# A fused retention and two-expert-layer kernel on one core: expert 0's raw-weight sums by ScalarE, PSUM and VectorE, x sums two a step, values asked for earlier, expert 3 staged by PSUM

## The chip, the cores and the metric

The kernel runs on one core of a Trainium2 chip. The metric is the device time in microseconds (us) of one execution. A core has five engines that each work through a queue of their own in order: TensorE (PE: matmuls, with its weight loads shown apart as PEld), VectorE (DVE), ScalarE (ACT), GpSimd (POOL) and SyncE (SP, which only issues transfers here). They share the on-chip buffer SBUF; matmuls write into PSUM.

## The reference, cut to what matters

Three layers follow on each other: causal retention, a dense layer of four experts, and a layer in which each token goes to the best of eight experts.

```python
def _attn_ref(q, k, v):                       # 4 x 8 heads x 576 x 64
    scores = scale * np.matmul(q, k.transpose(0, 1, 3, 2))
    Dmat = np.where(rel >= 0, gamma[:, None, None] ** rel[None, :, :], 0.0)
    return np.matmul(scores * Dmat[None, :, :, :], v)
def _moe_ref(x, domain_probs, w1, w2):        # x 2304 x 512, w1 4 x 512 x 1024
    p = domain_probs / (domain_probs.sum(-1, keepdims=True) + 1e-09)
    for e in range(E):
        out += p[:, e:e + 1] * (np.maximum(x @ w1[e], 0.0) @ w2[e])
def _moe2_ref(x, w_gate, w_output_gate, w1, w2):   # w1 8 x 512 x 1024
    logits = x @ w_gate; e_idx = np.argmax(logits, axis=1)
    gate_w = softmax(logits)[np.arange(N), e_idx]
    eom = 1.0 / (1.0 + np.exp(-(x @ w_output_gate)))
    for e in range(E):
        mask = e_idx == e
        out[mask] = gate_w[mask] * eom[mask, e] * (np.maximum(x[mask] @ w1[e], 0.0) @ w2[e])
```

## The kernel before, in words

**Numbers.** The expert layers multiply in f16. Each f32 value is split into a rounded f16 part `hi` and the f16 rest `lo = value - hi`, and a product takes three matmuls: hi x hi, hi x lo, lo x hi. The retention steps multiply in f32.

**Retention, 36 steps.** The sequence is cut into chunks of 64 tokens: 4 batches x 9 chunks are 36 steps. A step (`at_step`) multiplies the past state by the queries (L278), the next step's scores (L255, masked into `pf` by DVE, L260), `pf` by the values (L287), and makes the next state from `ks`, the keys weighted by POOL (`at_split`, L234), by the matmul L302. DVE adds the state up (`at_sum`, `sn`, L319) and scales the output into `xf` (L336); ACT writes its `hi` (L338), POOL its `lo` (L340; DVE, L342, for the first block). Queries, keys and values come by two transfers a step (`at_load`: `qkr`, `vkr`), four steps ahead in the opening, three later on.

**Blocks of x.** Four steps make a block of 256 tokens; there are nine. Each block also needs four differences of its quarters (`x_mix`, L348, POOL), which are split in their turn (`x_keep`: ACT L357, POOL L358, in two halves) and stored with the block (`x_store`, a POOL transfer, L361). A later part reads them back (`x_load`).

**The dense layer.** Expert 0 takes blocks 0 to 4 in the plain form (`l1_first`, L520, with `ht` by L506 on ACT and L507 on DVE; `l2`, L672, summing in PSUM tiles `po` of tag "o"). Everything later uses a seven-product form of the 2x2 block product: `l1_mixed` (L548) and `l2_mixed` (L633), whose seven products are added into `acc` by DVE (L641, weighted by `p_sb`), and whose left operands `op` get their `lo` from POOL (`whole`, L567). A block is up to 14 units of TensorE work. For the seven products the weights of an expert need sums and differences of their quarters: `mix`, L451, POOL, 16 per expert, made in place in the raw tile `wr`, between the splits `put` (`split_z`: ACT copies into a PSUM tile `pz`, L205, rounds it, L206, DVE subtracts, L207). Expert 0's sums are made while its own blocks 0 to 4 run.

**Hooks.** Between the units of expert 0 a hook runs one retention step (`at_hook`; steps 6 to 11 in block 0, eight each in blocks 1 to 3, four in block 4), `w_plan` runs one item of the list of weight sums and splits, and `s_plan` stages the second expert layer's weights: 128 pieces are read, split, and written back to DRAM as f16 pairs. For 46 of them `split_p` does it (L195, L196 on ACT, the difference L197 on POOL), for 82 `split_z`; expert 3's are by `split_p`. PSUM tiles `pz` are of tag "h" (shared with `ph`) or "o" (shared with `po`), two buffers each (`z_from`). From expert 3 on, the gating of the finished blocks runs too: `g1_rows` (L207 into `xr`), `g2` (L757), `g3a` (L767 to L774: maximum, key, one-hot), `g3b` (from L782; L808, L814), small DVE instructions of 128x16.

**Order.** A scheduler of the framework puts the instructions into each engine's queue; `pace` and `issue_after` hold the side work behind a given instruction of the main work. Within an engine the queue is strict.

```python
def split_p(raw, hi, lo, scale):
    act.activation(out=raw, in_=raw, func=ACTF.Copy, scale=scale)
    act.activation(out=hi, in_=raw, func=ACTF.Copy)
    pool.tensor_tensor(out=lo, in0=raw, in1=hi, op=ALU.subtract)
def split_z(raw, hi, lo, scale):
    z = z_at["bank"]().tile([128, 512], F32, tag=z_at["tag"], name="pz")
    act.activation(out=z, in_=raw, func=ACTF.Copy, scale=scale)
    act.activation(out=hi, in_=z, func=ACTF.Copy)
    dve.tensor_tensor(out=lo, in0=z, in1=hi, op=ALU.subtract)
```

Of the kernel before, what the change touches and what calls it, by code (L numbers as in the profile page):

```python
# [130 lines left out]
def kernel(  # L131
# [80 lines left out]
    at_ctx = ExitStack()  # L212
    at_raw = at_ctx.enter_context(tc.tile_pool(name="at_raw", bufs=4))
# [129 lines left out]

    def x_mix(b):

        m = xfs[b]
        for (ox, oy), x, y in (((0, 0), (1, 0), (0, 0)), ((1, 0), (1, 1), (1, 0)), ((1, 1), (1, 1), (0, 0)), ((0, 1), (0, 1), (1, 1))):
            pool.tensor_tensor(out=m[:, ox, oy], in0=m[:, x[0], x[1]], in1=m[:, y[0], y[1]], op=ALU.subtract)  # L348

    def x_keep(b):  # L350
        m = xfs.pop(b)
        if xos[b][1] is None:
            xos[b][1] = at_1.tile([128, 2, 4, 2, HB], F16, name="xm", bufs=1)
        with tc.issue_after(pace["act"].ins):
            for i in range(2):
                hi, lo = [xos[b][1][:, a, 2 * i:2 * i + 2] for a in range(2)]
                act.activation(out=hi, in_=m[:, i], func=ACTF.Copy)  # L357
                pool.tensor_tensor(out=lo, in0=m[:, i], in1=hi, op=ALU.subtract)  # L358

# [3 lines left out]
    def at_step(s):  # L363
# [10 lines left out]
        if s + 2 < NSTEP:
            at_split(s + 2)

    def at_done(s, f, *args):
        if s >= 0 and s % NS == NS - 1 and s < NSTEP:
            f(s // NS, *args)

# [772 lines left out]
    def at_hook():  # L1153
        s = nxt[0]
        if s >= NSTEP + 4:
            return
# [69 lines left out]
    def s_plan(e, b, u):  # L1226
        if e == 0 and b <= BM:
            if b == BM and u in (0, 2, 4, 6):
                s_hook()
        elif b >= 2:  # L1230
            if u in ((6, 13), (0, 3, 5, 7, 9), (0, 3, 5, 7, 9), (3, 5, 7, 9))[e] or u == 12 and (e == 3 and b < 5 or 0 < e < 3 and b >= 3):
                s_hook(split_z if 0 < e < 3 else split_p)
        elif b == 1 and u in (4, 6, 9):
            s_hook()

# [205 lines left out]
```

## Time and profile before

Three runs took 1009.95, 1010.9 and 1012.07 us, median 1010.9. The profiled execution took 1004.67 us; its span (first to last instruction of the trace) is 1002.9 us, its mean granted clock of TensorE 0.994.

| engine | busy us | share of the span | instructions |
|---|---|---|---|
| PE | 959.9 | 96% | 13507 |
| PEld | 825.7 | 82% | 13507 |
| DVE | 566.4 | 56% | 1251 |
| ACT | 525.6 | 52% | 1001 |
| POOL | 463.8 | 46% | 478 |

The page also cuts the span into 40 slices of 25.07 us, with each engine's busy share in tenths (9 is 90% or more). TensorE stands at 9 from the fourth slice on, until the last; in the first slices it is lower, and POOL is busiest there. Expert 0's plain blocks run in about the first 190 us, expert 3's blocks 3 to 7 begin at 633.27, 653.86, 674.46, 695.04 and 714.10 us, and the second expert layer ends the span. A releaser, named behind an arrow, is what ended the idle time in front of an instruction.

### The profile page before, as it was taken

The numbers are of one execution on the slowest core, as the hardware profiler recorded it, in microseconds if no ns is written. First come the engines' busy times: TensorE is split into PE (matmuls) and PEld (weight loads), VectorE is DVE, ScalarE is ACT, GpSimd is POOL, SyncE is SP. The second block draws the span as 40 slices with busy tenths as digits, with TensorE's granted clock in tenths as the row PEclk, the third lists the DMA queues.
The fourth block names the chain that finished last, engine by engine and source line by source line (L and its number), as shares of the span: only waits on it lengthen the run. The fifth ranks groups of instructions, "written<-read, shape, count | busy, mean of one in ns | idle before, by whom it ended". The sixth has DMA issues, their size and how long they took to land. (4 is left out here: it accounts for less than half of the span.)

```text
span 1002.9 us, 31867 instructions
## 1 busy us (share of the span) xinstructions
PE 959.9 (96%) x13507; PEld 825.7 (82%) x13507; DVE 566.4 (56%) x1251; ACT 525.6 (52%) x1001; POOL 463.8 (46%) x478
## 2 busy tenths in 40 slices
PE   5889999999999999999999999999999999999995
PEld 5566677899999999999999999888988677777773
DVE  5645461465677776766777774888798211211210
ACT  4235352677767777776787686576633122212221
POOL 3798973655555244454442554666543212112111
PEclk9999999999999999999999999999999999999998
DMA  9869884345457678476668636778945616554691
GB/s 343 291 221 324 269 269 156 108 119 185 164 187 219 224 260 275 122 212 215 207 195 318 226 96 164 207 214 235 222 143 202 232 44 220 203 227 143 255 397 44
DMA packets 95940, 209.49 MB, mean 209 GB/s; under 512 B 21486, under 2 KB 42222, under 8 KB 93488
## 3 DMA queue, kind: packets, MB, share of 16 engines
q1 hardware_dynamic: 82784, 159.20, 48.1%
q0 software_dynamic: 13008, 48.20, 15.0%
q8 instruction: 108, 1.77, 0.7%
q14 instruction: 40, 0.33, 0.1%
HBM read 197.88 MB, written 52.99 MB: 250 GB/s over the span
## 5 line engine op out<-in xcount | busy, mean ns | idle before, releaser
L633 PEld LDWEIGHTS <-op 128*128 128x128 f16 x2604 | 245.7, 98 | 30.3 <-issue 4.6
L567 POOL TENSOR_TENSOR op<-sm,op 128x512 f16<-128x512 f32 x124 | 142.2, 1157 | 180.2 <-ACT op L566 175.7
L548 PEld LDWEIGHTS <-wm_a 128*128 128x128 f16 x3264 | 192.8, 98 | 4.8 <-issue 1.0
L548 PE MATMUL ph<-xc,wm_a 128*128 128x128 f16 x2112 | 132.1, 219 | 0.0
L566 ACT ACTIVATE op<-sm 128x512 f16<-128x512 f32 x124 | 77.5, 633 | 83.6 <-DVE sm L571 83.6
L1055 DVE SCALAR_TENSOR_TENSOR h_s<-p_h,h_s 128x512 f16<-128x512 f32 x40 | 27.7, 692 | 158.4 <-ACT h_s L1054 151.2
L1062 PE MATMUL p_y<-wm_a,h_s 128*128 128x512 f16 x480 | 107.2, 379 | 0.5 <-DVE h_s L1055 0.5
L633 PE MATMUL pv<-wm_a,op 128*128 128x256 f16 x792 | 97.4, 273 | 0.0
L633 PE MATMUL px<-wm_a,op 128*128 128x256 f16 x744 | 91.5, 273 | 4.9 <-DVE acc L641 4.9
L451 POOL TENSOR_TENSOR wr<-wr 128x512 f32<-128x512 f32 x64 | 81.1, 1276 | 31.7 <-ACT pz L205 29.2
L1062 PEld LDWEIGHTS <-h_s 128*128 128x128 f16 x480 | 46.7, 98 | 52.4 <-DVE h_s L1055 0.7
L1065 POOL DMA_INDIRECT out_dram<-y_s,sidxm x17 | 17.2, 1014 | 146.4 <-ACT y_s L1064 137.8
L197 POOL TENSOR_TENSOR s<-sr,s 128x512 f16<-128x512 f32 x46 | 52.8, 1157 | 66.4 <-ACT s L196 62.2
L548 PEld LDWEIGHTS <-wm_b 128*128 128x128 f16 x1296 | 76.9, 98 | 1.4
L1054 ACT ACTIVATE h_s<-p_h 128x512 f16<-128x512 f32 x40 | 23.9, 597 | 78.5 <-PE p_h L1045 76.5
L641 DVE SCALAR_TENSOR_TENSOR acc<-px,p_sb,acc 128x256 f32<-128x256 f32 x124 | 59.2, 477 | 8.0 <-PE px L633 7.8
L1064 ACT ACTIVATE y_s<-p_y,x_g 128x512 f32<-128x512 f32 x20 | 13.7, 687 | 92.5 <-PE p_y L1062 74.3
L1045 PEld LDWEIGHTS <-wm_b 128*128 128x128 f16 x1056 | 59.9, 98 | 2.3
L1045 PE MATMUL p_h<-x_s,wm_b 128*128 128x128 f16 x1056 | 61.2, 219 | 0.0
L205 ACT ACTIVATE pz<-wr 128x512 f32<-128x512 f32 x100 | 59.4, 609 | 1.3 <-DVE wm_a L207 0.9
L207 DVE TENSOR_TENSOR s<-pz,s 128x512 f16<-128x512 f32 x82 | 54.7, 683 | 9.3 <-ACT s L206 9.3
L207 DVE TENSOR_TENSOR wm_a<-pz,wm_a 128x512 f16<-128x512 f32 x62 | 42.0, 689 | 28.8 <-ACT wm_a L206 27.9
(206 smaller groups left out, 1848.8 us busy)
## 6 DMA issues: line engine op xcount, KB each, us to landing
wm_a<-w2d SPq DMA_DIRECT2D x20, 2048.0 KB, 9.0
wr<-in_w_dram SPq DMA_DIRECT2D x40, 512.0 KB, 6.3
wm_b<-w1d SPq DMA_DIRECT2D x10, 2048.0 KB
wm_a<-w1d SPq DMA_DIRECT2D x10, 2048.0 KB
sr<-in_w1s_dram SPq DMA_DIRECT2D x64, 256.0 KB, 3.5
w1d<-s SPq DMA_DIRECT2D x64, 256.0 KB, 4.9
sr<-in_w2s_dram SPq DMA_DIRECT2D x64, 256.0 KB, 4.8
w2d<-s SPq DMA_DIRECT2D x64, 256.0 KB, 5.1
```

Source lines behind the costliest of these rows:

```text
L197: pool.tensor_tensor(out=lo, in0=raw, in1=hi, op=ALU.subtract)
L205: act.activation(out=z, in_=raw, func=ACTF.Copy, scale=scale)
L207: dve.tensor_tensor(out=lo, in0=z, in1=hi, op=ALU.subtract)
L451: pace["pool"] = pool.tensor_tensor(out=quarter(e, n, k, to), in0=quarter(e, n, k, x), in1=quarter(e, n, k, y), op=op)
L548: pe.matmul(bank[:, i], lhsT=w[:, k, u, 128 * i:128 * i + 128], rhs=x[:, v, d, k], start=(first and i == 0 and n == 0), stop=(n == 5), ski ...
L566: act.activation(out=hi, in_=s, func=ACTF.Copy)
L567: pool.tensor_tensor(out=lo, in0=s, in1=hi, op=ALU.subtract)
L633: pe.matmul(out, lhsT=o[a][:, v, k], rhs=w[c][:, k, u], start=(first and n == 0), stop=(n == 11), skip_group_check=True,)
L641: step = dve.scalar_tensor_tensor(out=a, in0=src, scalar=p_sb[:, b * TB + i, e:e + 1], in1=a, op0=ALU.mult, op1=ALU.add)
L1045: pe.matmul(ph[:, j], lhsT=w[k][:, x, f * 128:(f + 1) * 128], rhs=xs[:, y, k], start=(n == 0), stop=(n == 3 * KD - 1),)
L1055: dve.scalar_tensor_tensor(out=lo, in0=ph, scalar=0.0, in1=hi, op0=ALU.max, op1=ALU.subtract)
L1062: pe.matmul(po, lhsT=h[:, a, k], rhs=w[k][:, b], start=(n == 0), stop=(n == 3 * KF - 1))
```

## The change

1. `mix` for expert 0 no longer adds on POOL: ACT copies one quarter into a PSUM tile of the current tag, DVE adds or subtracts the other. Sixteen of the 64 sums.
2. `x_mix` makes two of its four differences a step, in the two steps behind the block's last; `x_keep` makes its two halves in the two steps after that, and the second store follows. `ago` counts the steps. The first block's, which stood at the end of the opening, come in the hooks of steps 6 to 10.
3. Values are asked for four steps ahead (`load_vk`, five buffers), queries and keys three (`load_qk`, four buffers); `at_split` stands ahead of `at_step` in the hook.
4. Expert 3's pieces of the staging (29) are split by `split_z`, and one of a block's hooks stands at unit 1 in place of 12. Expert 0's and those of block 1 of experts 1 to 3 stay with `split_p`.

```diff
+    def load_vk(s):
+        b, c = divmod(s, NC)
         t = at_raw.tile([128, 10, D], F32, name="vkr")
-        sp.dma_start(out=a[:, 0:10 if c else 8], in_=qk[b, c][:, 0:10 if c else 8])
...
-    def x_mix(b):
+    def x_mix(b, i):
...
+        for (ox, oy), x, y in steps[2 * i:2 * i + 2]:
             pool.tensor_tensor(out=m[:, ox, oy], in0=m[:, x[0], x[1]], in1=m[:, y[0], y[1]], op=ALU.subtract)
...
+    def ago(s, b):
+        return s - max(NS * b + NS - 1, NS + 1)
...
     def mix(e, n, k, to, x, y, op):
+        if e == 0:
+            z = z_at["bank"]().tile([128, 512], F32, tag=z_at["tag"], name="pz")
+            a, b, o = [quarter(e, n, k, i) for i in (x, y, to)]
...
+            act.activation(out=z, in_=a, func=ACTF.Copy)
+            dve.tensor_tensor(out=o, in0=z, in1=b, op=op)
+            return
...
     def opening(s):
         at_step(s)
+        at_split(s + 2)
+        load_vk(s + 4)
         if s < NS + 1:
-            at_load(s + 4)
+            load_qk(s + 4)
...
-    x_store(0, 0)
-    x_mix(0)
...
+        if s + 4 < NSTEP:
+            load_vk(s + 4)
         if s + 3 < NSTEP:
-            at_load(s + 3)
-        at_done(s - 1, x_mix)
+            load_qk(s + 3)
+        if s + 2 < NSTEP:
+            at_split(s + 2)
+        for b in range(NB):
+            if ago(s, b) == 1:
+                x_mix(b, 0)
         if s < NSTEP:
             at_step(s)
-        at_done(s - 2, x_store, 0)
-        at_done(s - 4, x_store, 1)
-        at_done(s - 3, x_keep)
+        for b in range(NB):
+            n = ago(s, b)
+            if n == 2:
+                x_store(b, 0)
+                x_mix(b, 1)
+            if 2 < n < 5:
+                x_keep(b, n - 3)
+            if n == (5 if b < NB - 1 else 4):
+                x_store(b, 1)
...
-    def s_hook(f=split_p):
+    def s_hook(f=split_z):
...
-            if u in ((6, 13), (0, 3, 5, 7, 9), (0, 3, 5, 7, 9), (3, 5, 7, 9))[e] or u == 12 and (e == 3 and b < 5 or 0 < e < 3 and b >= 3):
-                s_hook(split_z if 0 < e < 3 else split_p)
+            if u in ((6, 13), (0, 3, 5, 7, 9), (0, 3, 5, 7, 9), (3, 5, 7, 9))[e] or (e == 3 and b < 5 and u == 1) or (0 < e < 3 and b >= 3 and u == 12):
+                s_hook(split_z if e else split_p)
```

Lines move by 8 to 13: L234 becomes L242, L302 L310, L348 L357, L451 L462 (expert 0's on DVE), L520 L533, L633 L646, L641 L654, L769 L782.

POOL's queue at the end of the opening and in the first block, before: the `ks` are those of the retention steps, `wr` the raw weights of expert 0, `xf` the four x sums of a block, `xc` a `lo` part.

```order
L451 TENSOR_TENSOR wr<-wr 128x512 x4
L340 TENSOR_TENSOR xc<-xf,xc 128x4x64
L451 TENSOR_TENSOR wr<-wr 128x512 x2
L234 TENSOR_TENSOR ks<-vkr,ka 128x256
L451 TENSOR_TENSOR wr<-wr 128x512 x2
L348 TENSOR_TENSOR xf<-xf 128x256
L340 TENSOR_TENSOR xc<-xf,xc 128x4x64
L348 TENSOR_TENSOR xf<-xf 128x256
L361 DMA xcd<-xc 256x1x1024
L348 TENSOR_TENSOR xf<-xf 128x256
L234 TENSOR_TENSOR ks<-vkr,ka 128x256
```

The same stretch of POOL's queue now (L366 is the rounding rest of the halves of `x_keep`):

```order
L369 DMA xcd<-xc 256x1x1024
L357 TENSOR_TENSOR xf<-xf 128x256 x2
L242 TENSOR_TENSOR ks<-vkr,ka 128x256
L348 TENSOR_TENSOR xc<-xf,xc 128x4x64
L242 TENSOR_TENSOR ks<-vkr,ka 128x256
L348 TENSOR_TENSOR xc<-xf,xc 128x4x64
L366 TENSOR_TENSOR xc<-xf,xc 128x512
L242 TENSOR_TENSOR ks<-vkr,ka 128x256
L366 TENSOR_TENSOR xc<-xf,xc 128x512
L369 DMA xcd<-xc 256x1x1024
L348 TENSOR_TENSOR xc<-xf,xc 128x4x64
L242 TENSOR_TENSOR ks<-vkr,ka 128x256
```

The raw-weight sums have left this queue; between two `ks` stand a rounding rest or two and a transfer's issue.

DVE's queue at the end of the first-matrix units of block 1, before: `ht` of the last unit, the mask, a weight difference, the state and the output of a step.

```order
L507 SCALAR_TENSOR_TENSOR ht<-ph,ht 128x512
L260 TENSOR_TENSOR pf<-sc,ka 128x256
L207 TENSOR_TENSOR wm_a<-pz,wm_a 128x512
L319 SCALAR_TENSOR_TENSOR sn<-sn,ka,uo 128x64 x4
L336 TENSOR_TENSOR xf<-uo,ka 128x4x64
L207 TENSOR_TENSOR wm_a<-pz,wm_a 128x512 x2
```

The same place now:

```order
L520 SCALAR_TENSOR_TENSOR ht<-ph,ht 128x512
L268 TENSOR_TENSOR pf<-sc,ka 128x256
L462 TENSOR_TENSOR wr<-pz,wr 128x512
L327 SCALAR_TENSOR_TENSOR sn<-sn,ka,uo 128x64 x4
L344 TENSOR_TENSOR xf<-uo,ka 128x4x64
L207 TENSOR_TENSOR wm_a<-pz,wm_a 128x512
L268 TENSOR_TENSOR pf<-sc,ka 128x256
L207 TENSOR_TENSOR wm_a<-pz,wm_a 128x512 x2
```

A raw-weight sum, L462, stands now where a weight difference stood, ahead of the state; the difference has moved behind the output `xf`.

DVE's queue in expert 3 at the gating of a block (`lg`, `key`, `oh`: logits, key, one-hot), before:

```order
L641 SCALAR_TENSOR_TENSOR acc<-px_11788,p_sb,acc 128x256
L757 TENSOR_REDUCE lg<-pg 128x16
L767 TENSOR_REDUCE m<-lg 128x2
L769 TENSOR_TENSOR key<-lg,m 128x16
L808 TENSOR_TENSOR d<-lg,m 128x16
L770 TENSOR_TENSOR key<-key,kb 128x16
L772 TENSOR_REDUCE r<-key 128x2
L774 TENSOR_TENSOR oh<-key,r 128x16
L207 TENSOR_TENSOR xr<-pz,xr 128x512
L814 TENSOR_TENSOR g<-lg,oh 128x16
L816 TENSOR_REDUCE sg<-g 128x2
L641 SCALAR_TENSOR_TENSOR acc<-pv,p_sb,acc 128x256
```

The same block's gating now (`s` is a piece of the staging):

```order
L207 TENSOR_TENSOR s_12291<-pz,s_12291 128x512
L780 TENSOR_REDUCE m<-lg 128x2
L782 TENSOR_TENSOR key<-lg,m 128x16
L821 TENSOR_TENSOR d<-lg,m 128x16
L783 TENSOR_TENSOR key<-key,kb 128x16
L785 TENSOR_REDUCE r<-key 128x2
L787 TENSOR_TENSOR oh<-key,r 128x16
L827 TENSOR_TENSOR g<-lg,oh 128x16
L829 TENSOR_REDUCE sg<-g 128x2
L207 TENSOR_TENSOR xr<-pz,xr 128x512
L654 SCALAR_TENSOR_TENSOR acc<-pv,p_sb,acc 128x256
L207 TENSOR_TENSOR s_12352<-pz,s_12352 128x512
```

The chain L782 to L829 is the same; a staged difference stands ahead of it and one behind the sum into `acc`.

## Rows read from the trace of the kernel before

**Rows 1.** Waits of TensorE: engine line waited for: us in total, times, longest us.
```profile
PE uo L302 <- POOL ks L234: 6.9, 5, 2.6
PE px L633 <- DVE acc L641: 4.9, 4, 1.4
PE ph L520 <- DVE ht L507: 2.0, 1, 2.0
PE po L672 <- DVE xf L336: 1.6, 1, 1.6
```
**Rows 2.** Timeline of DVE: start, us, line operation, shapes, times [idle before, releaser].
```profile
26.96 2.35 DVE L192 SCALAR_TENSOR_TENSOR wm_c<-wr,wm_c 128x512 f16<-128x512 f32 x2
```
**Rows 3.** Timeline of POOL, 27 to 52 us.
```profile
27.61 3.42 POOL L348 TENSOR_TENSOR xf<-xf 128x256 f32<-128x256 f32 x3
...
42.34 5.39 POOL L451 TENSOR_TENSOR wr<-wr 128x512 f32<-128x512 f32 x4
...
50.88 0.61 POOL L234 TENSOR_TENSOR ks<-vkr,ka 128x256 f32<-128x256 f32 x1
```
**Rows 4.** Timeline of TensorE, 51 to 125 us.
```profile
51.55 0.46 PE L302 MATMUL uo<-vkr,ks 64*64 64x64 f32 x16 [1.71 <-POOL ks L234]
...
58.18 0.47 PE L302 MATMUL uo<-vkr,ks 64*64 64x64 f32 x16 [2.61 <-POOL ks L234]
...
76.94 2.76 PE L672 MATMUL po<-wm_c,ht 128*128 128x512 f16 x12
...
96.47 0.46 PE L302 MATMUL uo<-vkr,ks 64*64 64x64 f32 x16 [0.79 <-POOL ks L234]
...
124.23 0.46 PE L302 MATMUL uo<-vkr,ks 64*64 64x64 f32 x16 [1.36 <-POOL ks L234]
```
**Rows 5.** Stretches: length, PE, PEld, DVE, ACT, POOL busy (count), PEclk, DMA, GB/s.
```profile
58.00:60.00 2.00, 1.82 (x37) 1.45 (x38) 1.29 (x6) 1.70 (x5) 2.00 (x4) 0.63 0.94 361
60.00:62.00 2.00, 2.00 (x38) 1.40 (x35) 0.23 (x1) 1.23 (x4) 2.00 (x3) 0.52 0.05 19
```
**Rows 6.** Timeline of DVE in two blocks of expert 3.
```profile
635.00 3.45 DVE L769 TENSOR_TENSOR key<-lg,m 128x16 f32<-128x16 f32 x1
638.48 0.17 DVE L770 TENSOR_TENSOR key<-key,kb 128x16 f32<-128x16 f32 x1
...
696.86 1.15 DVE L808 TENSOR_TENSOR d<-lg,m 128x16 f32<-128x16 f32 x1
...
698.33 0.81 DVE L774 TENSOR_TENSOR oh<-key,r 128x16 f16<-128x16 f32 x1
...
699.75 0.51 DVE L814 TENSOR_TENSOR g<-lg,oh 128x16 f32<-128x16 f32 x1
...
701.25 0.48 DVE L641 SCALAR_TENSOR_TENSOR acc<-px,p_sb,acc 128x256 f32<-128x256 f32 x1
```
**Rows 7.** Timeline of POOL beside the first of these blocks.
```profile
635.03 1.16 POOL L197 TENSOR_TENSOR s<-sr,s 128x512 f16<-128x512 f32 x1
```
**Rows 8.** Timeline of TensorE behind the sum at 701.25.
```profile
701.78 1.47 PE L633 MATMUL px<-wm_a,op 128*128 128x256 f16 x12
```
**Rows 9.** Groups by line: shapes, times, busy us, mean ns, idle before, releaser.
```profile
L451 POOL TENSOR_TENSOR wr<-wr 128x512 f32<-128x512 f32 x64 | 81.1, 1276 | 31.7 <-ACT pz L205 29.2 <-DMA wr<-in_w_dram 1.2
...
L205 ACT ACTIVATE pz<-wr 128x512 f32<-128x512 f32 x100 | 59.4, 609 | 1.3 <-DVE wm_a L207 0.9 <-DVE wm_c L207 0.3
...
L207 DVE TENSOR_TENSOR s<-pz,s 128x512 f16<-128x512 f32 x82 | 54.7, 683 | 9.3 <-ACT s L206 9.3
...
L197 POOL TENSOR_TENSOR s<-sr,s 128x512 f16<-128x512 f32 x46 | 52.8, 1157 | 66.4 <-ACT s L196 62.2 <-DMA w1d<-s 4.0
```
**Rows 10.** The page's slices: busy tenths of 25.07 us each.
```profile
DVE  5645461465677776766777774888798211211210
ACT  4235352677767777776787686576633122212221
```
**Rows 11.** Timeline of ACT at the end of block 1's first units.
```profile
75.95 0.60 ACT L506 ACTIVATE ht<-ph 128x512 f16<-128x512 f32 x1 [0.61 <-PE ph L520]
```

More of the change, by code (lines that the diff above doesn't have):

```diff
@@ L212 @@
     at_ctx = ExitStack()
-    at_raw = at_ctx.enter_context(tc.tile_pool(name="at_raw", bufs=4))
+    at_raw = at_ctx.enter_context(tc.tile_pool(name="at_raw", bufs=5))
     at_1 = at_ctx.enter_context(tc.tile_pool(name="at_1", bufs=3))
@@ L217, with load_qk @@
     ka = at_1.tile([128, ca.shape[1]], F32, name="ka", bufs=1)
-    raws, pm, st, uos, pace = {}, {}, {}, {}, {}
+    qks, raws, pm, st, uos, pace = {}, {}, {}, {}, {}, {}
     xcs, xfs, xos = {}, {}, {}
     def at_load(s):
+        load_qk(s)
+        load_vk(s)
+    def load_qk(s):
         b, c = divmod(s, NC)
-        a = at_raw.tile([128, 10, C], F32, name="qkr")
+        a = at_raw.tile([128, 10, C], F32, name="qkr", bufs=4)
+        pace["sp"] = sp.dma_start(out=a[:, 0:10 if c else 8], in_=qk[b, c][:, 0:10 if c else 8])
+        qks[s] = a
+    def load_vk(s):
+        b, c = divmod(s, NC)
         t = at_raw.tile([128, 10, D], F32, name="vkr")
-        sp.dma_start(out=a[:, 0:10 if c else 8], in_=qk[b, c][:, 0:10 if c else 8])
         pace["sp"] = sp.dma_start(out=t[:, 0:4 if c == NC - 1 else 10], in_=vk[b, c][:, 0:4 if c == NC - 1 else 10])
-        raws[s] = a, t
+        raws[s] = (t,)
     def at_split(s):
@@ L234, in at_split @@
             pool.tensor_tensor(
-                out=ks, in0=raws[s][1][:, 4:8], in1=cst("ktab", 4, 1).to_broadcast([128, 4, D]), op=ALU.mult
+                out=ks, in0=raws[s][0][:, 4:8], in1=cst("ktab", 4, 1).to_broadcast([128, 4, D]), op=ALU.mult
             )
@@ L249, in at_scores @@
     def at_scores(s):
-        a = raws[s][0]
+        a = qks[s]
         sc = at_ps[-1].tile([128, 2, 512], F32, tag="sc", name="sc", bufs=1)
@@ L274, in at_past @@
             return
-        sn, q, uo = st[s - 1], raws[s][0], uos[s][0]
+        sn, q, uo = st[s - 1], qks[s], uos[s][0]
         for h in HEADS:
@@ L283, in at_b @@
     def at_b(s):
-        t, uo, pf = raws.pop(s)[1], uos[s][0], pm.pop(s)
+        t, uo, pf = raws.pop(s)[0], uos[s][0], pm.pop(s)
         for h in HEADS:
@@ L297, in at_state @@
             return
-        t, ks = raws[s][1:3]
+        t, ks = raws[s]
         uo = uos[on][0]
@@ L342, in at_out, with x_keep @@
             dve.tensor_tensor(out=lo, in0=xf, in1=hi, op=ALU.subtract)
-    def x_mix(b):
+    def x_mix(b, i):
         m = xfs[b]
-        for (ox, oy), x, y in (((0, 0), (1, 0), (0, 0)), ((1, 0), (1, 1), (1, 0)), ((1, 1), (1, 1), (0, 0)), ((0, 1), (0, 1), (1, 1))):
+        steps = ((0, 0), (1, 0), (0, 0)), ((1, 0), (1, 1), (1, 0)), ((1, 1), (1, 1), (0, 0)), ((0, 1), (0, 1), (1, 1))
+        for (ox, oy), x, y in steps[2 * i:2 * i + 2]:
             pool.tensor_tensor(out=m[:, ox, oy], in0=m[:, x[0], x[1]], in1=m[:, y[0], y[1]], op=ALU.subtract)
-    def x_keep(b):
-        m = xfs.pop(b)
+    def x_keep(b, i):
+        m = xfs[b]
         if xos[b][1] is None:
@@ L354, in x_keep @@
         with tc.issue_after(pace["act"].ins):
[L355 to L358, printed above, removed]
+            hi, lo = [xos[b][1][:, a, 2 * i:2 * i + 2] for a in range(2)]
+            act.activation(out=hi, in_=m[:, i], func=ACTF.Copy)
+            pool.tensor_tensor(out=lo, in0=m[:, i], in1=hi, op=ALU.subtract)
     def x_store(b, i):
@@ L373, in at_step @@
         at_out(s)
[L374 to L379, printed above, removed]
+    def ago(s, b):
+        return s - max(NS * b + NS - 1, NS + 1)
     def x_load(b, q, base=False):
@@ L450, in mix @@
     def mix(e, n, k, to, x, y, op):
+        if e == 0:
+            z = z_at["bank"]().tile([128, 512], F32, tag=z_at["tag"], name="pz")
+            a, b, o = [quarter(e, n, k, i) for i in (x, y, to)]
+            if len(a.shape) == 3:
+                z = z.rearrange("p (k d) -> p k d", k=a.shape[1])
+            act.activation(out=z, in_=a, func=ACTF.Copy)
+            dve.tensor_tensor(out=o, in0=z, in1=b, op=op)
+            return
         pace["pool"] = pool.tensor_tensor(out=quarter(e, n, k, to), in0=quarter(e, n, k, x), in1=quarter(e, n, k, y), op=op)
@@ L1228, in s_plan @@
             if b == BM and u in (0, 2, 4, 6):
[L1229 removed]
+                s_hook(split_p)
         elif b >= 2:
[L1231 to L1232 removed]
+            if u in ((6, 13), (0, 3, 5, 7, 9), (0, 3, 5, 7, 9), (3, 5, 7, 9))[e] or (e == 3 and b < 5 and u == 1) or (0 < e < 3 and b >= 3 and u == 12):
+                s_hook(split_z if e else split_p)
         elif b == 1 and u in (4, 6, 9):
[L1234 removed]
+            s_hook(split_p)
     gate = []
```

## The prediction

> **What bounds the kernel now.** I read the waits of TensorE first. Most of the span it has no idle time, so only its gaps and its clock can be won or lost by a change that leaves its matmuls as they are. The reader is to see four lines [rows 1]: 6.9 us in five waits for `ks` from GpSimd (POOL), 4.9 us in four for the weighted sum that VectorE (DVE) writes into `acc`, one of 2.0 us for `ht` and one of 1.6 us for `xf`, both from DVE. Then the timelines show who made these late.
>
> In the opening, DVE's differences L192 stand one after the other at 1.2 us each (2.35 for two [rows 2]), while POOL runs three x sums L348 from 27.61 to 31.03 [rows 3]. Outside that stretch an L192 takes 0.68 (estimate: the PSUM form L207 of the same size, 0.69 [rows 9]). So the x sums on POOL stretch DVE by about 0.53 each, four times, and the 2.0 us wait follows.
>
> At 42.34 POOL begins four raw-weight sums L451 in one piece of 5.39 us, more follow, and the `ks` of step 10 begins at 50.88 only [rows 3]. TensorE waits 1.71 for it at 51.55, 2.61 at 58.18, and 0.79 and 1.36 later on [rows 4]: 6.47 together. From 58 to 62, right behind the two long gaps, the granted clock is 0.63 and 0.52 [rows 5], so at the lower level of 1.2 GHz for most of it: (0.37 + 0.48) x 2 us = 1.70 us lost. What TensorE did before is the gap of 2.61.
>
> In expert 3 the routing instruction L769 takes 3.45 us at 635.00, where its neighbour L770 of the same 128x16 size takes 0.17 [rows 6]: a hold of 3.28, which began as POOL began a run of L197, L567, L197 the first in [rows 7]. It comes in three blocks, and in each the sum behind it reaches TensorE about 1.45 late (three of the four waits of [rows 1]). In the next block POOL has a gap between these, three smaller holds remain (1.15, 0.81 and 0.51, less 0.17 each: 1.96 [rows 6]), and the sum L641 that began at 701.25 with 0.48 ends at 701.73; TensorE's matmul starts at 701.78 without a wait [rows 8]. So there is no slack there either.
>
> **The change part by part.** The sum is made against the profiled execution, 1004.67 us; the median of the runs shown, 1010.9, is 6.2 above it, and I carry that difference over.
>
> *Opening.* The x sums of the first block go behind all the `ks` of the opening, so four L192 lose 0.53 each (2.1), and the 2.0 wait goes. Not all of it stays won: in the new order the moved sums start where DVE still has its last two L192 to do, which can cost 2 x 0.53 again ahead of the `xf` that TensorE waits for next (the 1.6 wait), and the first weight sums now stand on DVE ahead of a state update and wait for weights from DRAM. Bounds: 0 (all given back to the next wait) and 3.6 (both waits go). I take 1.5, nearer the row of the wait that is surely hit, less half of one hold.
>
> *Expert 0's sums off POOL, and the x sums two a step.* Sixteen of the 64 L451 go: 16 x 1.28 = 20.4 us of POOL [rows 9], eight of them from the very run that delays `ks`. In the new order of POOL nothing of the kind stands ahead of those `ks`, and the one that was 1.36 late stands one piece of work earlier. What is next late there is the half-tile rounding L366 that waits for ACT, with about 1 us to spare by the old times. Bounds: 4.3 (only the two long waits go) and 6.9 (also the 0.47 one in the opening, which nothing here touches). I take the four, 6.5, and with them the clock's 1.7 (bounds 0 and 1.7; no gap of 2 us is left near it).
>
> *What the sums cost in their new place.* Each adds an ACT copy to PSUM, about 0.61 as L205, and a DVE instruction, about 0.69 as L207 [rows 9]: 9.7 and 11.0 us in a stretch (25 to 150 us, the slices two to six of the page) where DVE is busy for four to six tenths and ACT for two to five [rows 10], so the time itself is hidden; what counts is who queues behind. On DVE a sum stands ahead of the state update `sn` (behind it the `xf`), for which TensorE's next L278 waits. At the last L520 unit of the second block TensorE went on to `po` at 76.94 [rows 4] while ACT had only begun the `ht` copy at 75.95 [rows 11]. Now two PSUM buffers of tag "o" are both held by a difference and a sum there: ACT does `ht` (0.60), one L365 (about 0.6), two copies (1.2), so the second copy ends near 78.2; DVE's sum ends at 78.9, and `po` starts 1.6 later than it could (3.3, if it gets the buffer of the difference, which stands behind `sn`, and `xf`). The four sums of the second matrices that come together on DVE in the third block take 4 x 0.69 = 2.8 in a row, while no row shows how early the next `sn` is; I take 0.8 of it as a hold (bounds 0 and 2.8), and 0.1 each at four other places. Together -2.5. Bounds: +0.3 (the buffers come free in time) and -20.8 (each of 16 costs the whole pair, 1.30).
>
> *Expert 3's 29 differences off POOL.* That is 29 x 1.16 = 33.6 us of POOL and 29 x 0.68 = 19.8 us more on DVE [rows 9]; on ACT two passes stay two passes. In the three blocks with the long hold, only one L567 is left near L769, so a hold of up to 1.15 stays (the row of L808 [rows 6]). In two of them two new differences stand between the old ones ahead of the sum: 3.28 - 1.15 - 2 x 0.68 = 0.77 won each; in the third one difference: 1.45 won, the whole wait. In the two blocks after: 1.96 - 1.15 - 0.68 = +0.13, so no new wait. Sum 2.9. Bounds: 4.9 (all four waits go) and -2.6 (nothing won, and the two blocks without slack pay 1.30 each).
>
> The Trainium skill, page "SBUF — State Buffer", section "Who interferes with whom", says that a DVE instruction with two SBUF inputs and a GpSimd one that reads SBUF exclude each other for a whole instruction, and that one with at most one SBUF input is not held. By that rule the moved sums and differences, with one input in PSUM, are never held, and the L567 that stay go on holding L769 and its like. The trace agrees that L207 stays at 0.68; it does not agree on one instruction's length, for L769 was held through POOL's whole run of three, 3.28. Were each of the two inputs' instructions held once more by one L567, nothing would be won in expert 3, which is the second rival below.
>
> *At nothing:* values asked for a step earlier (the same transfers; the fifth buffer lets them go out, and the `ks` waits were POOL's, not a transfer's); the second half of each x block stored one step later (it is read again several steps on); the hook moved from unit 12 to 1 (the same number a block). If that cover went, one transfer's landing would stand in the path once.
>
> Sum: 1.5 + 6.5 + 1.7 - 2.5 + 2.9 = 10.1 us. Profile 994.6, median 1000.8.
>
> **The rivals.** (a) *All waits go and the new ones don't come*: for it, every wait above has its cause in work that moves; against it, the PSUM buffers. 3.6 + 6.5 + 1.7 + 0.3 + 4.9 = 17.0: 993.9. (b) *DVE becomes the bound in expert 3*: for it, the blocks without slack; against it, that DVE is left with fewer holds than the differences cost. Expert 3 gives -1.3 for +2.9: 5.9 won, 1005.0. (c) *The change does not reach `ks`*: the sums leave, but `ks` stays late since POOL waits for ACT's rounding, which now stands behind four copies to PSUM. The 6.5 and 1.7 fall away: 1.9 won, 1009.0, no difference that counts. (d) *Slower*: the DVE queue, in order, is held by the sums. Place: expert 0's blocks 0 to 3; each sum waits for an ACT copy that is itself behind `ht` copies and roundings, and `pf` and `sn` behind it are what TensorE needs next in the step. Price: 16 x 1.30 = 20.8, and 3.3 more at `po`: 24.1 against the 12.6 that the other terms win: 11.5 slower, 1022.4. It decides from an average of 12.6 / 16 = 0.8 us a sum. Against it: DVE's share of four to six tenths there [rows 10]: a queue with that much idle time seldom holds the next instruction for as long as the pair lasts.
>
> **How the numbers follow.** Forecast 0.62, (a) 0.13, (b) 0.13, (c) 0.06, (d) 0.06. The forecast's own range is 997 to 1005. The range from 994.9 to 1007.5 holds the forecast, (b) and most of (a), and leaves out (c), (d) and the end of (a): about 0.16. A measurement of this kernel tells 0.2%, some 2 us, from no change. Faster by more than that: forecast, (a), (b): 0.87, one of a hundred taken off for the far end of (b). Within it: (c) and that, 0.07. Slower: (d), 0.06.
>
> **What would show it.** Right: no wait for `ks` over 0.3 us behind 40 us, and the granted clock at 1.00 from 50 to 75; L192 near 0.7 before 31 us; waits of the matmul L646 for `acc` under 2.5 us in total; L782 at 1.2 or less; a wait of 1 to 3.5 us for `po` at the first second-matrix unit of the second block. Wrong step by step: `ks` still late behind 45 us (c); L286 waiting for `sn` or L295 for `pf`, over 4 us in total (d); more and longer waits for `acc` in blocks 3 to 7 of expert 3 (b). The forecast itself is wrong if the time is above 1005 or below 997.

## The result, and the profile after

The changed kernel took 1002.12 us (median of 6 runs, 998.31 to 1005.17) against 1010.22 (6 runs of the kernel before, 1008.58 to 1012.07): ratio 0.9917, 95% interval 0.9890 to 0.9944, so 8.4 us off (2.7 either way). The forecast was 10.1 off. The profiled execution took 998.96 us, 5.7 less than that of before. Of all executions in this document one, of 1664.41 us in the run with the sums alone, is left out of the ratios.

The page's busy times now (us, share of the span, instructions), for the table of before:

```profile
PE 960.9 (96%) x13507; PEld 827.5 (83%) x13507; DVE 577.3 (58%) x1296; ACT 534.2 (54%) x1017; POOL 411.7 (41%) x433
```

POOL has 52 us less, and DVE only 11 more. By the prediction's rows DVE was given 11.0 + 19.8 = 30.8 us of new work, so (an estimate) some 20 us of what it was busy with before were holds that are gone. Where TensorE waits now, as in [rows 1] (the first lines; four waits for the first transfers of `qkr` lead both lists):

```profile
PE sc L263 <- DMA qkr<-in_qk_dram: 10.2, 4, 3.4
PE uo L286 <- DVE xf L344: 2.1, 3, 0.9
PE sc L263 <- DVE pf L268: 2.1, 2, 1.3
PE ph L533 <- DVE ht L520: 2.0, 1, 2.0
...
PE po L685 <- DVE wr L462: 0.7, 1, 0.7
PE px L646 <- DVE acc L654: 0.7, 2, 0.5
```

The 6.9 for `ks` (but for 0.5 in the opening) and most of the 4.9 for `acc` are gone; the 2.0 for `ht` is not, and 4.2 stands for `xf` and `pf` ahead of the retention matmuls, where before it was 0.7. The 1.6 of `po` for `xf` is gone too, for a reason of its own, shown with the clock below. First the opening, POOL's timeline and DVE's (start, us, instruction, times, [idle before]):

```profile
26.27 1.04 POOL L357 TENSOR_TENSOR xf<-xf 128x256 f32<-128x256 f32 x1 [0.77 <-DVE xf L344]
27.74 0.73 POOL L357 TENSOR_TENSOR xf<-xf 128x256 f32<-128x256 f32 x1 [0.42 <-DVE xc L350]
28.41 0.88 POOL L369 DMA_DIRECT2D xcd<-xc  x1
29.22 1.98 POOL L357 TENSOR_TENSOR xf<-xf 128x256 f32<-128x256 f32 x2
31.17 1.06 POOL L242 TENSOR_TENSOR ks<-vkr,ka 128x256 f32<-128x256 f32 x1
```
```profile
28.19 2.44 DVE L192 SCALAR_TENSOR_TENSOR wm_c<-wr,wm_c 128x512 f16<-128x512 f32 x2
30.55 2.23 DVE L192 SCALAR_TENSOR_TENSOR wm_a<-wr,wm_a 128x512 f16<-128x512 f32 x2
```

All four x sums of block 0 still run here, ahead of the `ks` at 31.17, and L192 is as long as in [rows 2]. Next TensorE's timeline from 33 to 115 us, all its waits over 0.3 us but one of 0.54 at 102.79:

```profile
33.16 0.49 PE L533 MATMUL ph<-xc,wm_c 128*128 128x128 f16 x6 [2.00 <-DVE ht L520]
...
46.16 0.46 PE L286 MATMUL uo<-qkr,sn 64*64 64x64 f32 x16 [0.88 <-DVE xf L344]
...
48.75 0.44 PE L263 MATMUL sc<-qkr 64*64 64x64 f32 x10 [1.35 <-DVE pf L268]
...
73.26 0.46 PE L286 MATMUL uo<-qkr,sn 64*64 64x64 f32 x16 [0.31 <-DVE xf L344]
...
75.16 0.46 PE L263 MATMUL sc<-qkr 64*64 64x64 f32 x16 [0.74 <-DVE pf L268]
76.35 2.75 PE L685 MATMUL po<-wm_c,ht 128*128 128x512 f16 x12 [0.73 <-DVE wr L462]
...
114.47 0.46 PE L286 MATMUL uo<-qkr,sn 64*64 64x64 f32 x16 [0.91 <-DVE xf L344]
```

None of [rows 4]'s waits for `ks` is left; 4.92 us of new ones stand in their stead, 2.23 of them near 46 to 49. What made those late, on ACT and on DVE:

```profile
42.47 1.12 ACT L461 ACTIVATE pz<-wr 128x512 f32<-128x512 f32 x2 [2.05 <-DMA wr<-in_w_dram]
46.52 1.12 ACT L461 ACTIVATE pz<-wr 128x512 f32<-128x512 f32 x2 [2.94 <-DMA wr<-in_w_dram]
```
```profile
47.68 0.69 DVE L462 TENSOR_TENSOR wr<-pz,wr 128x512 f32<-128x512 f32 x1 [1.67 <-ACT pz L461]
48.28 0.41 DVE L268 TENSOR_TENSOR pf<-sc,ka 128x256 f32<-128x256 f32 x1
```

ACT waits for raw weights from DRAM, the sum L462 waits 1.67 for ACT, and `pf`, next in DVE's queue, starts behind the sum. The granted clock (seventh value of a stretch) fell at other places than in [rows 5]:

```profile
16.00:18.00 2.00, 1.62 (x37) 1.20 (x38) 2.00 (x8) 0.42 (x1) 0.32 (x1) 0.68 1.05 408
18.00:20.00 2.00, 2.00 (x22) 2.00 (x20) 1.34 (x5) 1.15 (x2) 0.85 (x1) 0.50 1.04 420
...
34.00:36.00 2.00, 2.00 (x41) 1.80 (x42) 1.93 (x5) 0.94 (x3) 1.27 (x1) 0.50 0.17 54
36.00:38.00 2.00, 2.00 (x63) 1.88 (x58) 1.81 (x9) 0.00 (x0) 0.84 (x2) 0.70 0.43 109
...
58.00:60.00 2.00, 2.00 (x60) 1.64 (x58) 1.03 (x4) 0.42 (x1) 2.00 (x4) 1.00 0.89 256
```

58 to 62 us is at 1.00 now, but two stretches are at the lower level, 1.2 GHz: (0.32 + 0.50) x 2 = 1.6 us, and (0.50 + 0.30) x 2 = 1.6, 3.2 in all against 1.7 in the execution of before. The second of the two cost nothing further. It lies where TensorE had waited 1.63 for `xf`, and now TensorE comes to `po` that much later and finds `xf` written. First before, then now:

```profile
37.63 2.76 PE L672 MATMUL po<-wm_c,ht 128*128 128x512 f16 x12 [1.63 <-DVE xf L336]
```
```profile
38.72 2.76 PE L685 MATMUL po<-wm_c,ht 128*128 128x512 f16 x12
```

So the wait for `xf` was covered by the slow stretch and not removed: with the `ht` wait unchanged, `po` starts 1.1 later than before, which the first fall alone gives (in it 46 matmuls L533 from 17.76 take 3.85 us, before 2.74). The pages add up with this. TensorE's waits, as they are listed without those for the first transfers, come to 20.7 us before and 13.5 now; 7.2 less, and 1.5 more lost to the clock, make 5.7, beside the 5.9 by which the spans differ (1002.9 and 997.0). Each kernel has one trace, so this sum holds for the two profiled executions, not for the 8.4 of the medians.

Expert 3, DVE and then POOL, beside [rows 6] and [rows 7]:

```profile
632.88 0.68 DVE L207 TENSOR_TENSOR s<-pz,s 128x512 f16<-128x512 f32 x1
...
633.67 0.76 DVE L782 TENSOR_TENSOR key<-lg,m 128x16 f32<-128x16 f32 x1
```
```profile
633.23 1.16 POOL L580 TENSOR_TENSOR op<-sm,op 128x512 f16<-128x512 f32 x1
```

The hold of 3.28 is 0.59 (0.76 less 0.17), here and in the four blocks behind it: one L580 was left, and it had already run for 0.44. One later block still holds the line L821 for 0.97 (1.13 less 0.16, at 728.37). The three waits of 1.45 are gone.

### The profile page after: what moved, and what is told of

The parts are those of the page before. It is cut to its first block, busy times and chain, and to the rows that moved or that the text cites. A ratio compares the mean times of both kernels' runs of the same rounds, so it can differ in the third digit from the quotient of the medians.

```text
span 997.0 us, 31905 instructions
## 1 busy us (share of the span) xinstructions
PE 960.9 (96%) x13507; PEld 827.5 (83%) x13507; DVE 577.3 (58%) x1296; ACT 534.2 (54%) x1017; POOL 411.7 (41%) x433
## 5 line engine op out<-in xcount | busy, mean ns | idle before, releaser
L646 PEld LDWEIGHTS <-op 128*128 128x128 f16 x2604 | 245.6, 98 | 26.0 <-POOL s L197 0.7
L580 POOL TENSOR_TENSOR op<-sm,op 128x512 f16<-128x512 f32 x124 | 142.2, 1157 | 223.9 <-ACT op L579 223.8
L646 PE MATMUL pv<-wm_a,op 128*128 128x256 f16 x792 | 97.4, 273 | 0.0
L646 PE MATMUL px<-wm_a,op 128*128 128x256 f16 x744 | 91.3, 272 | 0.7 <-DVE acc L654 0.7
L207 DVE TENSOR_TENSOR s<-pz,s 128x512 f16<-128x512 f32 x111 | 74.0, 683 | 15.6 <-ACT s L206 15.6
L205 ACT ACTIVATE pz<-sr 128x512 f32<-128x512 f32 x111 | 65.6, 605 | 14.4 <-DVE rk L804 8.8
L464 POOL TENSOR_TENSOR wr<-wr 128x512 f32<-128x512 f32 x48 | 60.4, 1270 | 29.9 <-ACT pz L205 29.2
L1067 ACT ACTIVATE h_s<-p_h 128x512 f16<-128x512 f32 x40 | 23.9, 597 | 78.9 <-PE p_h L1058 74.9
L206 ACT ACTIVATE s<-pz 128x512 f16<-128x512 f32 x111 | 64.0, 599 | 0.6
L654 DVE SCALAR_TENSOR_TENSOR acc<-px,p_sb,acc 128x256 f32<-128x256 f32 x124 | 59.2, 478 | 7.3 <-PE px L646 7.0
```

Source lines behind the costliest of these rows:

```text
L580: pool.tensor_tensor(out=lo, in0=s, in1=hi, op=ALU.subtract)
L646: pe.matmul(out, lhsT=o[a][:, v, k], rhs=w[c][:, k, u], start=(first and n == 0), stop=(n == 11), skip_group_check=True,)
L654: step = dve.scalar_tensor_tensor(out=a, in0=src, scalar=p_sb[:, b * TB + i, e:e + 1], in1=a, op0=ALU.mult, op1=ALU.add)
```

## The experiments

Ratios are to runs of the kernel before on the same chip, with the 95% interval; the kernel before had a median of 1009.1 to 1011.0 us in each set.

**Sums back on POOL.**
```diff
-        if e == 0:
+        if e < 0:
             z = z_at["bank"]().tile([128, 512], F32, tag=z_at["tag"], name="pz")
```


> The changed kernel with one part undone: expert 0's sixteen raw-weight sums are made by GpSimd again. Theory 1 (the sums were what made ks late, and on VectorE they now hold pf, sn and xf in their turn): TensorE waits for ks again for 4 us or more in total behind 40 us, the waits for pf and xf near 46 and 48 us go, and the time is 2 to 4 us above the changed kernel, ratio to before about 0.995. Theory 2 (ks is early because its call now stands ahead of the step, and the sums on VectorE are pure cost): no wait for ks over 0.5 us, and 3 to 5 us less than the changed kernel, ratio about 0.987.

Measured 0.9922 (0.9899 to 0.9945): the time of the changed kernel. The waits for `xf` and `pf` near 46 to 49 went, and one for `ks` came:
```profile
64.38 0.71 PE L310 MATMUL uo<-vkr,ks 64*64 64x64 f32 x16 [4.13 <-POOL ks L242]
```
Behind it the clock was at 0.50 from 64 to 70 us. The wait of `po` for `xf` stands at 1.62 here, at 38.92, where this execution's clock did not fall ahead of it. Theory 1 is right on what waits, not on the time; theory 2 is wrong on both.

**Expert 3 staged as before.**
```diff
-... or (e == 3 and b < 5 and u == 1) or (0 < e < 3 and b >= 3 and u == 12):
-                s_hook(split_z if e else split_p)
+... or u == 12 and (e == 3 and b < 5 or 0 < e < 3 and b >= 3):
+                s_hook(split_z if 0 < e < 3 else split_p)
```


> The changed kernel with one part undone: expert 3's pieces are staged as before, differences on GpSimd, hook at unit 12. Theory 1 (in expert 3 the change won 4.8 us, as the sums into acc show, which stand 1.8 us earlier than before ahead of it and 6.6 behind it): the holds of the routing line of 128x16 (3.4 us) come back in three blocks, waits for acc of 4 to 5 us, ratio to before about 0.9965. Theory 2 (the extra differences on VectorE fill what the holds leave, as the prediction's second rival had it): the same time as the changed kernel within 1 us, ratio about 0.992.

Measured 0.9964 (0.9941 to 0.9986): 4.7 us above the changed kernel (0.0047 of 1010; 3.6 either way, by both intervals), theory 1. The waits for `acc` are back at 4.3, and DVE shows the hold again (the hook's move from unit 12 to 1 is undone with it and was not run alone):
```profile
634.33 3.45 DVE L782 TENSOR_TENSOR key<-lg,m 128x16 f32<-128x16 f32 x1
```

**x sums of block 0 behind the last `ks` of the opening, that of step 7.**
```diff
+            pace["ks"] = pool.tensor_tensor(          # in at_split
...
             if ago(s, b) == 1:
-                x_mix(b, 0)
+                with tc.issue_after(pace["ks"].ins):
+                    x_mix(b, 0)
```


> The changed kernel, and block 0's four x sums are queued on GpSimd behind the ks of step 8, so that they leave the opening (in the changed kernel they still run from 26.3 to 31.2 us there). Theory 1 (the x sums stretch the differences of line L192 and so make ht late): L192 takes 0.7 us in place of 1.2 between 28 and 33 us, the wait of 2.0 us for ht falls under 0.5, and the time is 1.5 to 3 us under the changed kernel. Theory 2 (something else stretches them, such as the transfer that GpSimd issues or the weights' arrival): L192 stays over 1.1 us and the wait stays at 2.0. Theory 3: the wait goes, and the next one (po for xf) takes it back: no gain behind 40 us.

Step 8 is the last chunk of its batch and makes no `ks`; the instruction that the edit names, and behind which POOL runs the sums here, is the `ks` of step 7.

Measured 0.9882 (0.9855 to 0.9910): 3.5 us under the changed kernel, with intervals that overlap. L192 takes 0.64 and the wait for `ht` went; the next, of `po` for `xf`, is 2.78 (1.63 before): theories 1 and 3 each in part. Its profiled execution was a long one (1004.62 us; in it TensorE stands still for 2.77 ahead of 151.98, and the profile names nothing that it waits for), so the place of the gain is read from the two like it below.

**Sums two units later.**
```diff
-[w_loads(0, 0, 2), w_loads(0, 1, 3)] + w1_steps(0)
+[w_loads(0, 0, 2), w_loads(0, 1, 3)] + [lambda: None] * 2 + w1_steps(0)
```


> The changed kernel with two empty items put into the list between expert 0's weight loads and its first sums, so that the sums start two units later. Theory 1 (the first sums wait for weights from DRAM, ACT at 42.5 and 46.5 us, and hold pf and xf behind them on VectorE): the waits of 0.9 us for xf and 1.35 for pf near 46 and 48 us and the late xf go, worth 3 to 3.7 us at 48 us, and the time is 2 to 4 us under the changed kernel. Theory 2 (a sum holds the queue wherever it stands): the waits come back in the second block, and the time stays within 1 us.

Measured 0.9943 (0.9922 to 0.9965): 2.6 us slower than the changed kernel, with intervals that overlap. The waits at 46 to 49 did go, and a larger one came at the start of the third block. TensorE, DVE and ACT there:
```profile
87.49 0.46 PE L263 MATMUL sc<-qkr 64*64 64x64 f32 x16 [4.09 <-DVE pf L268]
```
```profile
85.29 0.69 DVE L207 TENSOR_TENSOR wm_a<-pz,wm_a 128x512 f16<-128x512 f32 x1 [5.92 <-ACT wm_a L206]
```
```profile
83.32 0.63 ACT L365 ACTIVATE xm<-xf 128x512 f16<-128x512 f32 x1 [4.57 <-DMA xcd<-xm]
```
The rounding of an x half waits for the store that still reads the one tile `xm`; a weight's rounding stands behind it on ACT, its difference waits on DVE, and `pf` behind that: three queues in order, and a transfer at the end. Both theories missed this chain. One more wait, of 1.86 for `xf`, came at 155.49.

**Values three steps ahead, `ks` behind the step.** `load_vk` and `load_qk` of the hook become one `at_load(s + 3)`, four buffers, and `at_split(s + 2)` goes behind `at_step(s)`.

> The changed kernel with one part undone: values asked for three steps ahead with four buffers, ks made behind the step, as before. Theory 1 (this part is worth nothing, as the prediction put it, since ks was late for GpSimd's sums and not for a transfer): no wait for ks over 0.6 us behind 40 us, the time of the changed kernel within 1 us, ratio to before about 0.992. Theory 2 (the sums of expert 0 on VectorE bring nothing, as the run with the sums back on GpSimd has the same time, because it is the earlier ks that counts): waits for ks of 3 us or more in total, ratio 0.995 or more.

Measured 0.9919 (0.9895 to 0.9944): theory 1, no wait for `ks` over 0.3 behind 40 us.

**x sums grouped as before.**
```diff
             if ago(s, b) == 1:
                 x_mix(b, 0)
+                x_mix(b, 1)
...
-            if 2 < n < 5:
-                x_keep(b, n - 3)
-            if n == (5 if b < NB - 1 else 4):
+            if n == 3:
+                x_keep(b, 0), x_keep(b, 1)
+            if n == 4:
```


> The changed kernel with one part undone: the four x sums of a block in one step, its two half-tile roundings in one step, its second store one step earlier, as before. Theory 1 (the later second store keeps the one tile xm busy, so that the rounding into it waits on ACT: 6.5 us at 150 us in the changed kernel against 2.1 before): the waits of ACT for the store of xm fall under 3 us, and the time is 1 to 2 us under the changed kernel. Theory 2 (two sums a step spare ks): waits for ks come back near 80 and 115 us, and the time is 1 to 2 us above it. Theory 3: no difference that can be measured.

Measured 0.9920 (0.9897 to 0.9943): theory 3. ACT's longest wait for the store of `xm` fell from 6.5 to 3.3 us, a wait of 1.27 behind POOL came at 102.73, and the time stayed.

**Grouped as before, and behind the `ks` of step 7.** The edits of the third and the sixth run together.

> The changed kernel with the x sums, roundings and stores of a block grouped as before, and the first block's sums queued behind the ks of step 8, so out of the opening. Theory 1 (leaving the opening is worth 3 us, as the run with late sums alone showed, and the grouping adds what the run with the old grouping shows): ratio 0.987 to 0.989, the wait of 2.0 us for ht gone. Theory 2 (four sums in one piece of about 3 us ahead of the next ks make it late): a wait for ks of 1 us or more between 38 and 50 us, ratio 0.990 or more.

Measured 0.9908 (0.9885 to 0.9931): the ratio of theory 2 without the wait that it named, for no `ks` was late between 38 and 50 us. The wait for `ht` is gone; the sums now run beside the last pair of L192, the wait of `po` for `xf` is 2.54, and one of 1.92 behind POOL's L366 came at 101.79. POOL, then DVE:
```profile
30.68 3.79 POOL L357 TENSOR_TENSOR xf<-xf 128x256 f32<-128x256 f32 x4
```
```profile
31.06 2.03 DVE L192 SCALAR_TENSOR_TENSOR wm_a<-wr,wm_a 128x512 f16<-128x512 f32 x2
```

**The sums alone, on the kernel before.** Only the branch `if e == 0:` of `mix` is added.

> The kernel before with one part of the change alone: expert 0's sixteen raw-weight sums by ACT, PSUM and VectorE. Theory 1 (the prediction's term: ks waits of 6.5 us and a clock dip of 1.7 go, holds of 2.5 come): no wait for ks over 0.5 us behind 40 us, 5 to 6 us less than before, ratio about 0.9945. Theory 2 (the holds of pf, sn and xf on VectorE, above all behind sums that wait for weights from DRAM, take back all of it): no wait for ks either, but waits for pf and xf of 4 us or more in total, ratio 0.998 to 1.001.

Measured 0.9960 (0.9943 to 0.9977): 4.0 us (1.7 either way), between the two. No wait for `ks` behind 40 us, but 2.73 at 49.55 and 1.35 at 78.17 for `pf`, and 0.83 for `xf` at 117.07, 4.9 in these three, as theory 2 had it:
```profile
49.55 0.44 PE L255 MATMUL sc<-qkr 64*64 64x64 f32 x10 [2.73 <-DVE pf L260]
...
78.17 0.34 PE L255 MATMUL sc<-qkr 64*64 64x64 f32 x8 [1.35 <-DVE pf L260]
```

**x sums of block 0 behind the next `ks`, that of step 9.** As the third run, with `(1 if b else 2)` for the first half.

> The changed kernel, with block 0's four x sums queued one step later still than in the run with late sums, behind the ks of step 9. Theory 1 (x sums on GpSimd stretch whichever L192 they run beside, in the run before the last pair from 31 us, so that xf and with it po were 2.5 us late): all L192 from 26 to 34 us take 0.7 us, the wait for ht stays gone and the wait of po for xf falls under 1.7 us, ratio to before 0.986 to 0.989. Theory 2 (the wait of po for xf is set by the count of instructions on VectorE, not by their stretch): it stays at 2.5 us, ratio 0.989 to 0.991.

Measured 0.9867 (0.9841 to 0.9892), median 998.02 us: the fastest, 5 us (3.7 either way) under the changed kernel. The x sums leave the opening, L192 takes 0.64 each, and `po` waits 1.78, at 36.23:
```profile
31.16 0.61 POOL L242 TENSOR_TENSOR ks<-vkr,ka 128x256 f32<-128x256 f32 x1 [2.99 <-DMA vkr<-in_vk_dram]
...
36.12 3.18 POOL L357 TENSOR_TENSOR xf<-xf 128x256 f32<-128x256 f32 x4
```
```profile
27.53 1.28 DVE L192 SCALAR_TENSOR_TENSOR wm_c<-wr,wm_c 128x512 f16<-128x512 f32 x2
28.73 1.29 DVE L192 SCALAR_TENSOR_TENSOR wm_a<-wr,wm_a 128x512 f16<-128x512 f32 x2
```
Theory 1, but for 0.1 us at `po`: the last pair, beside one L348 at 31.98, was still at 1.76.

**The same, first sums one unit later.** One `lambda: None` in place of two.

> The same with one empty item ahead of expert 0's first sums, so that these start one unit later, where the run with two empty items alone was 2.6 us slower than the changed kernel. Theory 1 (the first sums then find their weights landed, and one unit is not enough to push the second matrix's items into the waits at 83 us): the waits for pf and xf from 43 to 50 us fall under 0.5 us in total, 1 to 2 us under the run without the empty item. Theory 2 (every unit of delay moves a split beside the x rounding of the next block, where ACT stands): a wait for pf of 2 us or more near 85 us, and 1 to 2 us above it.

Measured 0.9900 (0.9872 to 0.9927): not better. The wait for `xf` near 44 did not go (1.91 at 44.22, where the run above has 1.28), and none of 2 us near 85 came (0.60 at 83.62); one of 2.12 for `xf` came at 149.48, with the clock at 0.50 behind it. Neither theory, and against the run above it can't be told from no difference.

**x sums and values alone, on the kernel before.** Made as the first two edits of this section together, on the changed kernel.

> The kernel before with the x sums' steps, the values four steps ahead and the earlier ks alone: expert 0's sums on GpSimd and expert 3's staging as before. Theory 1 (the parts add up: the sums alone won 4.0 us and expert 3 4.7, which is the whole gain): ratio 0.999 to 1.001. Theory 2 (the earlier ks wins part of what the sums also win, so that undoing the sums showed nothing): ratio 0.996 to 0.998, with one or two waits for ks instead of four.

Measured 0.9994 (0.9978 to 1.0011): theory 1, though two waits for `ks` instead of four, as theory 2 had it. The second is as long as those it replaces; on POOL two roundings and a sum stand ahead of that `ks`:
```profile
66.12 0.70 PE L310 MATMUL uo<-vkr,ks 64*64 64x64 f32 x16 [4.18 <-POOL ks L242]
```
```profile
61.32 2.27 POOL L366 TENSOR_TENSOR xc<-xf,xc 128x512 f16<-128x512 f32 x2
63.55 1.25 POOL L464 TENSOR_TENSOR wr<-wr 128x512 f32<-128x512 f32 x1
64.76 0.67 POOL L369 DMA_DIRECT2D xcd<-xc  x1
65.39 0.68 POOL L242 TENSOR_TENSOR ks<-vkr,ka 128x256 f32<-128x256 f32 x1
```

**Tag h at unit 3 of block 1**, on the fastest: `u >= 3` for `u >= 4` in the loop's `z_from`.

> The kernel with block 0's x sums behind the ks of step 9, and the sum and difference that stand at unit 3 of block 1 take PSUM tiles of tag h in place of o, so that po does not share with them. Theory 1 (the prediction's term: po waits because both tiles of tag o are held): the wait of 0.73 us of po for the sum goes, at most 0.7 us off, which the time cannot tell (ratio to before 0.984 to 0.989). Theory 2 (the sum then waits for ph to be read, stands later in the queues, and holds sn and the next pf): a wait of 1 us or more moves to the next matmuls of the step, and the time is 0 to 2 us above the kernel without this.

Measured 0.9883 (0.9856 to 0.9910), the same within the intervals. `po` starts at 72.55 with no wait:
```profile
72.17 0.44 PE L310 MATMUL uo<-vkr,ks 64*64 64x64 f32 x16
72.55 2.76 PE L685 MATMUL po<-wm_c,ht 128*128 128x512 f16 x12
```
So that wait went, as theory 1 has it, and the tiles of tag "o" are its likely cause, since the trace names the sum L462 as what ended it. The run is not a clean proof: TensorE's order changed with it, and the scores L263 that stood ahead of `po` with a wait of 0.74 for `pf` now stand behind it. The wait for `pf` of 1.08 at 84.23 is new.

## Why the prediction was right, and where it was not

The time came as forecast, 8.4 for 10.1 us, and the parts add up by runs of their own: sums 4.0 (added alone to the kernel before), expert 3 4.7, x sums and values 0.6, together 9.3, each with some 2 to 4 us either way. Taken out of the changed kernel, the sums show only 0.5 (see *Open*). The terms were not all sized right, and one failed; that the total is near is in part luck, for the opening's 1.5 that was not won and the 2.4 by which the sums cost more are partly made up by the 1.8 more from expert 3.

*Opening, 1.5: failed.* The step that said the x sums "go behind all the `ks` of the opening" is wrong. The code puts them into later hooks, but the queue has them ahead of the `ks` of step 7, as the order of POOL shows in its second row; the place in the code was read for the place in the queue. So nothing was won: L192 at 1.2, the wait of 2.00 still there. What the step said of the cause holds: once the sums do leave, L192 falls to 0.64, the wait for `ht` goes and the next one (`po` for `xf`) stays. That one follows the last pair of L192: with the x sums beside it the pair takes 2.26 or 2.03 and `po` waits 2.78 or 2.54; with one L348 beside it, 1.76 and 1.78, or 1.28 and 1.15 in the two runs (the last, and the one with the first sums one unit later) in which the L348 is the one that was held, 1.53 for 0.67. The version behind step 9's `ks` is 5 us faster than the changed kernel, though the intervals touch, at 0.989; its `po` starts at 36.23 in place of 38.72, which is 2.5 of it, and where the rest comes from was not found in one execution's trace. The size was also a little high: by [rows 2] an L192 was stretched by 1.18 - 0.68 = 0.50, not 0.53.

*`ks`, 6.5, and the clock, 1.7.* The waits went as put, 6.47 to 0.54. The clock's part did not: in 58 to 62 it is at 1.00, but it fell twice elsewhere. In twelve of the fourteen traces here the clock fell ahead of TensorE's last matmul, behind a gap or a thin stretch near 16, 33, 40, 44, 50, 58, 64, 72, 88 or 150 to 160 us, not behind the same ones each time, and in two it did not. A gap that is taken away need not give back a fixed 1.7.

*The sums' new place, -2.5: too small.* In the trace it is up to 4.92; the run with the sums back on POOL still has two waits for `xf`, of 0.42 and 0.45, so some 4.0 of it (an estimate) are the sums' own. The term was also added up wrong: its parts, 1.6 and 0.8 and four times 0.1, make 2.8, and by its own times (78.9 after 76.94) the first would be 2.0. Of the prediction's own places, `po` waited 0.73 for 1.6 (see the last run), and `xf` and `pf` beside it 1.05. A later step adds 0.91 at 114, where DVE has four sums ahead of it. What it did not have is the first sums' weights: 2.23 us near 46 to 49, where ACT waits 2.05 and 2.94 for that transfer, and DVE holds `xf` and `pf` meanwhile. By the run with the sums alone, what was put at 6.5 + 1.7 - 2.5 = 5.7 measured 4.0 (1.7 either way), at the edge of its interval.

*Expert 3, 2.9 (its parts make 3.0): measured 4.7,* near the upper bound 4.9; the trace shows 4.3. The hold that remains is 0.59 and not up to 1.15 - 0.17, and the new differences took room that DVE had, so the whole 1.45 was won in each of three blocks (4.34), not 0.77 in two. By the rule on the page "SBUF — State Buffer" of the Trainium skill, section "Who interferes with whom", the differences with one input in PSUM should not be held; all 111 L207 of the staging take 0.68 to 0.69, some of them with a POOL instruction beside them for nearly all of that, so the trace agrees.

*At nothing:* borne out for the values and the grouping, each undone with no difference beyond some 3.6 us either way, and both alone at 0.9994 (1.7 us either way). The hook's move was not tested by itself.

*Rivals.* (c) is out by the trace, (b) by the run on expert 3. (d), the sums holding DVE, is real at 4.92 of its 24.1: 0.3 us a sum, where it decides from 0.8. (a) came in expert 3 alone.

*Open.* Undoing the sums from the changed kernel cost 0.5 us, while alone they win 4.0. The intervals (some 3.5 and 1.7 either way) overlap, so this may be noise; why the earlier `ks` and halved x sums should win about 3 us with the sums on POOL in one kernel and nothing in the other, with the same wait of 4.1 us, was not found.

## What to carry to other kernels

Read the place of a moved instruction in its engine's queue and not in the code, above all where a scheduler stands between; one line that queues it behind a named instruction was worth as much here (5 us, 3.7 either way) as the largest part of the change (4.7). Work moved from an idle engine to one that feeds TensorE takes its waits along: see which transfer it waits for, and what stands behind it. Short DVE instructions that read SBUF and take many times their length are worth a look at what GpSimd does beside them.

## What the hardware showed that was not expected

TensorE's clock does not fall behind the same gap each time: behind the wait of 2.03 us for `ht` it stayed at 1.00 in the trace of before, and fell behind one of 2.00 in that of the changed kernel, for some 3 us at half speed. Seven traces have this gap, at 2.00 to 2.03: the clock fell behind it in the five in which it had also fallen near 16 us, and not in the two in which it had not. Executions of one kernel spread over up to 11 us (998.31 to 1005.17 the changed kernel, 994.04 to 1004.62 the one with late x sums); the mean granted clock goes with it in part, 0.996 in the changed kernel's fastest execution and 0.991 in its slowest.

The granted clock of a stretch is not always the pace of the matmuls in it: in both traces whose clock did not fall, it stands at 1.00 from 16 to 18 us, and sixteen L310 that begin at 16.11 and 16.18 take 0.70 there, where the same sixteen take 0.41 to 0.46 later on.

A transfer issued by GpSimd beside L192 did not stretch it: 27.27 to 28.16 in the fastest version, L192 at 0.64.
